# Half of the second layer's output projection moved into its attention, with the last two groups of heads taking turns

## The chip, the cores and the metric

The kernel runs on one core of a Trainium2 chip. The core has a matrix engine (TensorE, in the profile PE, with its weight loads as PEld), three engines for elementwise work (VectorE or DVE, ScalarE or ACT, GpSimd or POOL) and SyncE (SP), which here only issues DMAs. Every engine works through its own list of instructions in order; engines wait for each other by semaphores. The metric is the device time of one execution in microseconds (us).

## The reference

Four layers on an x of 2048 rows by 640 channels: attention, a state space convolution, attention, the convolution, each on a layer normalisation of x and each added to x. The attention has 32 heads of 20 channels.

```python
q, k, v = qkv[0], qkv[1], qkv[2]
scores = jnp.einsum("bhqd,bhkd->bhqk", q, k) * (Dh ** -0.5)
p = _softmax(scores, axis=-1)
o = jnp.einsum("bhqk,bhkd->bhqd", p, v)
return (lambda x, *d: x.transpose(*d))(o, 0, 2, 1, 3).reshape(B, S, D) @ wo
...
x = x + _A_ref(_layernorm(x, axis=-1), A_wqkv, A_wo)
x = x + _B_ref(_layernorm(x, axis=-1), B_log_A_real, B_A_imag, B_C_real, B_C_imag, B_log_dt, B_D_skip)
```

The product with wo is the output projection of the title: for each block of 128 rows, 640 channels of o (five channel tiles of 128) go into 640 columns, in two halves of 320.

## The kernel before, in words

**Attention** (`attention`, from L394) is made for two layers, one call each. The heads go in eight groups of four (L930), a group's queries in four blocks of 512 (L932), and for each block the keys in 16 tiles of 128 (L942). A key tile is two *scores* (L817: eight small matmuls on 64 x 32 pieces of PE's array, then one exponential of 128 x 1024 on ACT, L827, into `pt`) and one *values* (L833: the product of `pt` with V, summed in PSUM as `pa` over the 16 key tiles). A row of ones in V gives the softmax's denominator. There are 1024 exponentials in a layer.

At the end of a block of queries (L844 to L890) DVE adds the two halves of `pa` into `oc`; the denominators then go out and back: POOL stores them (`sums`, dn<-oc), loads them spread over the partitions (`load`, dr<-dn), DVE inverts them (`invert`), POOL stores and spreads them (`back`, dn<-dr; `spread`, db<-dn), DVE multiplies (`scale`) and POOL stores the result into `ot` in DRAM (`store`, ot<-oc). These steps are put off by planned times (L886: 0.2, 5, 10, 11 and 15.5 us after the block); `scale` comes when the next block of queries ends (L854).

Keys and queries are kept as operands in SBUF: `kop[j][half]` (two pairs of heads, two halves of the keys) and `qop[j][parity]`. `load_k` (L409) and `load_q` (L418) let SP load them from DRAM: the second half of the keys and the next queries at key tile 2 of a block (L949), the first half and the queries of the next group at key tile 10 of a group's last block (L955), after `need` has made sure that the group's projections are done.

**The order of the work** is set by a plan with a clock for PE, ACT and DVE (`Plan`, L50): scores cost PE 0.22 us and ACT 0.92 (L828), values cost PE 0.865 (L836). What is left of PE's time is filled from generators of small steps: `slot` (L672) takes the next step of `todo` when it fits before the planned end of the exponential under way less 0.5 us (L922). In the first layer a second source, the convolution's kernel (`pend`, from `kgen`), fills too; `AHEAD` (L33, L659) says how much of the first must be done at which exponential before the second is taken. The steps of `todo` are the projections of the other groups (`jobs`, L557: `qk` for queries and keys, `vq` for values, `both` to interleave them), and `fetch` (L605) loads the weights for them through one staging buffer `ws`: it turns what was staged into weights on DVE, and in the same call lets SP load the next. Within the attention each engine's order is fixed as written (`Ordered`, L62, and `chain`, L179, for PE). After it, instructions can be moved ahead of others on their engine.

When the projections are over, `end_jobs` (L892) frees their buffers, loads wo and lets POOL split it into two parts, `woh` and `wol` (`prefetch`, L972).

**The output projection** (`out_proj`, L1092) follows the attention: for each of 16 blocks of 128 rows, `out_split` (L994) loads the columns of `ot` (otl<-ot), rounds them (`oh`, on ACT) and takes the rest (`ol`, on DVE); 30 matmuls (two halves, five channel tiles, ol x woh, oh x woh, oh x wol) go to PSUM, and DVE adds the result to x. For two blocks at a time the layer normalisation follows (`ln_stats` L139, `ln_u` L1013): statistics and u on DVE, `uh` on ACT, `ul` on POOL. Then the convolution (`ssm`, L1128) begins with psx (L1163). Rows 12 to 15 belong to the last block of queries.

Of the kernel before, what the change touches and what calls it, by code (L numbers as in the profile page):

```python
# [32 lines left out]
AHEAD = ((0, 0.0), (110, 6.0), (236, 34.0), (364, 61.0), (600, 95.0), (740, 134.0))  # L33
# [51 lines left out]
def mha_s4d_kernel(ctx, tc, x_in, wqkv, wo, lar, aim, cr, ci, ldt, dsk,  # L85
# [48 lines left out]
    with tc.tile_pool(name="op", bufs=1) as op:  # L134
        oneh = op.tile([1, L], F16, name="oneh")
        ge.memset(oneh, 1.0)
        ge.dma_start(onesd, oneh)

# [255 lines left out]
    def attention(x, stats):  # L394
# [23 lines left out]
        def load_q(g, j, qb):  # L418

            qt = qop[j][qb % 2]  # L420
# [136 lines left out]
        def jobs():  # L557
# [59 lines left out]
            def vq(q):  # L617
                w = wv_.pop()
# [95 lines left out]
        with ExitStack() as c2:  # L714
# [82 lines left out]
            for j in range(2):  # L797
                load_k(0, j, 0)
                load_q(0, j, 0)
# [15 lines left out]
        ready, scaled = [], []  # L815
# [17 lines left out]
        def values(qb, g, kt, pts, pa):  # L833
# [10 lines left out]
            if kt == NI - 1:  # L844
# [9 lines left out]
                if scaled:  # L854
                    scaled.pop()()
# [26 lines left out]
                def store():  # L882
                    for j in range(4):
                        h = 4 * g + j
                        ge.dma_start(ot[h * DH:(h + 1) * DH, 512 * qb:512 * qb + 512], oc[32 * j:32 * j + DH, :])
                later.extend((plan.dve + n, f) for n, f in (  # L886
                    (0.2, sums), (5.0, load), (10.0, invert), (11.0, back), (15.5, spread)))
                later.extend((plan.dve + n, lambda: slow and slow.pop(0)[1]()) for n in (18.0, 21.0, 24.0))
                later.sort(key=lambda e: e[0])
                scaled.append(scale)  # L890
# [35 lines left out]

        last[0] = None
        tail = None
        every = {NBLK - 1, ("v", 3)}
        for g in range(H // 4):  # L930
            need(NEED[g], ("v", g // 2))
            for qb in range(4):  # L932
                if g == H // 4 - 1 and qb == 3:
                    if tail is None:
                        need(*every)
                        tail = end_jobs()
                    split, fetch = out_split(tail[-1], 1 if first_layer else 2)
                    first = []
                    later.extend(((plan.pe + 7.0, fetch), (plan.pe + 20.0, lambda: first.append(split(0)))))
                    later.sort(key=lambda e: e[0])  # L940
                pa = [pst("A", [P, 512], F32, tag=f"pa{r}", name=f"pa{r}") for r in range(2)]
                for kt in range(NI):  # L942
                    kc, pts = P * (kt % 8), []
                    for j in range(2):
                        pts.append(scores(kop[j][kt // 8], kc, qop[j][qb % 2]))
                        if j:
                            ready.append((plan.act, qb, g, kt, pts, pa))
                        fill(j)
                    if kt == 2:  # L949
                        for j in range(2):  # L950
                            if qb == 0:
                                load_k(g, j, 1)
                            if qb < 3:
                                load_q(g, j, qb + 1)
                    if qb == 3 and kt == 10 and g + 1 < H // 4:  # L955
                        need(NEED[g + 1])
                        for j in range(2):
                            load_k(g + 1, j, 0)
                            load_q(g + 1, j, 0)
                if tail is None and filler[0] is None and have.issuperset(every):  # L960
                    tail = end_jobs()
        for r_ in ready:
            values(*r_[1:])
        drain_later(True)
        scaled.pop()()
        drain_later(True)
        plan.keep = False
        first.append(split(1))
        c.close()
        return *tail[:-1], split, first  # L970
# [23 lines left out]
    def out_split(w2, n):  # L994

        def load(s):
            o = w2.tile([P, NCT, P], F32, name="otl")
            sy.dma_start(o, ot[:, s * P:s * P + P].rearrange("(t p) c -> p t c", p=P))
            return o
        o = []  # L1000

        def split(s):
            oh = w2.tile([P, NCT, P], F32R, name="oh")
            ol = w2.tile([P, NCT, P], F32R, bufs=n, name="ol")
            cur = o.pop(0)
            (ve.tensor_copy if s == 0 else se.copy)(oh, cur)
            ve.tensor_sub(ol, cur, oh)
            if s + 1 < NI:
                o.append(load(s + 1))
            return oh, ol  # L1010
        return split, lambda: o.append(load(0))

    def ln_u(x, i0, n, mvrs, uh, ul, pool):  # L1013
        mv, rs = mvrs
        for i in range(n):
# [76 lines left out]
    def out_proj(x, woh, wol, split, first, ln):  # L1092
        for s in range(NI):
            oh, ol = first.pop(0)
            pos = [pst("M", [P, 512], F32, tag="mm", name="po")[:, :320] for _ in range(2)]
            for hf in range(2):
                for ct in range(NCT):
                    te.matmul(pos[hf], ol[:, ct, :], woh[:, ct, 320 * hf:320 * hf + 320], start=(ct == 0), stop=False)  # L1098
            if s + 2 < NI:
                first.append(split(s + 2))  # L1100
            for hf in range(2):
                for ct in range(NCT):
                    for m in (woh, wol):
                        te.matmul(pos[hf], oh[:, ct, :], m[:, ct, 320 * hf:320 * hf + 320],  # L1104
                                  start=False, stop=(ct == NCT - 1 and m is wol))
                xs = x[:, s, 320 * hf:320 * hf + 320]
                ve.tensor_add(xs, xs, pos[hf])
                if s == 2:
                    weave(1000)
# [237 lines left out]
    def seq(x, general):  # L1347

        stats = None
        for n in range(0, len(parts), 2):  # L1350
            with ExitStack() as c:
# [4 lines left out]
                else:  # L1356
                    x, wc, *tail = attention(x, stats)
                psum(c, X=2)
# [9 lines left out]
                with ExitStack() as c2:  # L1368
                    up2 = c2.enter_context(tc.tile_pool(name="up2", bufs=2))

                    def ln(i0, m):
                        ln_u(x, i0, m, ln_stats(lambda i: x[:, i0 + i, :], m), uh, ul, up2)
# [97 lines left out]
```

## Time and profile before

| what | value |
|---|---|
| median of 3 runs | 2721.36 us (2717.77 to 2724.57) |
| the profiled execution | 2718.84 us |
| its span, first to last instruction | 2717.1 us |
| PE busy | 2534.4 us (93% of the span) |
| ACT busy | 2337.4 us (86%) |
| DVE busy | 1477.0 us (54%) |
| POOL busy | 852.6 us (31%) |
| exponentials of the first layer | 115.5 to 1099.8 us |
| exponentials of the second layer | 1503.5 to 2485.5 us |
| second layer's output projection on PE | 2488.3 to 2558.8 us |

Rows of the profile name a line, an engine, an operation and its operands as out<-in; a number in brackets is the time that the engine stood idle before, with the engine that ended it. L77 is the line of the helper `Ordered`, which issues most instructions of ACT, DVE, POOL and SP, so these are told apart by their operands. SPq and POOLq rows are DMA issues.

### The profile page before, as it was taken

The numbers are of one execution on the slowest core, as the hardware profiler recorded it, in microseconds if no ns is written. First come the engines' busy times: TensorE is split into PE (matmuls) and PEld (weight loads), VectorE is DVE, ScalarE is ACT, GpSimd is POOL, SyncE is SP. The second block draws the span as 40 slices with busy tenths as digits, with TensorE's granted clock in tenths as the row PEclk, the third lists the DMA queues.
The fourth block names the chain that finished last, engine by engine and source line by source line (L and its number), as shares of the span: only waits on it lengthen the run. The fifth ranks groups of instructions, "written<-read, shape, count | busy, mean of one in ns | idle before, by whom it ended". The sixth has DMA issues, their size and how long they took to land.

```text
span 2717.1 us, 115609 instructions
## 1 busy us (share of the span) xinstructions
PE 2534.4 (93%) x50944; PEld 1445.2 (53%) x50944; DVE 1477.0 (54%) x3292; ACT 2337.4 (86%) x2762; POOL 852.6 (31%) x1282
## 2 busy tenths in 40 slices
PE   7899999999999988999999999899999998888998
PEld 3445444444444433777886445444445443335988
DVE  7777877778856970577776332232232220003865
ACT  7899999999999999455655899899999999997464
POOL 1132333333333343301670122222223223222376
PEclk9999999999999999999999999999999999999999
DMA  6522222232222232455542111111121112112365
GB/s 214 174 62 75 63 77 64 73 75 61 65 51 59 51 112 87 145 210 194 178 142 67 45 52 52 50 53 46 46 66 35 50 36 61 41 38 80 110 191 161
DMA packets 183153, 238.55 MB, mean 88 GB/s; under 512 B 42737, under 2 KB 128241, under 8 KB 180849
## 3 DMA queue, kind: packets, MB, share of 16 engines
q1 hardware_dynamic: 146304, 184.48, 21.0%
q0 software_dynamic: 36336, 46.59, 7.2%
q8 instruction: 402, 6.59, 1.0%
q14 instruction: 111, 0.90, 0.1%
HBM read 154.90 MB, written 76.03 MB: 85 GB/s over the span
## 4 chain that ended last, share of the span: by engine, by line
ACT 49%; PE 30%; issue 9%; DVE 7%; DMA 4%; POOL 1%; SPq 0%; ACTq 0%; DVEq 0%; POOLq 0%
ACT pt L77 47%; PE pa L841 5%; PE S L824 3%; PE psv L1198 3%; PE po L1104 3%; PE psy L1208 2%; PE m L578 2%; PE psx L1186 2%; PE psx L1163 2%; PE po L1098 1%; PE pst L1173 1%; PE pkf L1078 1%; DMA kop<-ks 1%; PE pv L544 1%; PE pq L730 1%
## 5 line engine op out<-in xcount | busy, mean ns | idle before, releaser
L77 ACT ACTIVATE pt<-S 128x1024 f32<-128x1024 f32 x2048 | 1922.9, 1037 | 46.7 <-PE S L824 37.1
L841 PE MATMUL pa<-pt,V 64*32 64x512 f32 x16384 | 1101.0, 590 | 0.9 <-DVE oc L77 0.8
L824 PE MATMUL S<-qop,kop 61*32 61x512 f16 x16384 | 880.4, 381 | 125.4 <-ACT pt L77 105.1
L824 PEld LDWEIGHTS <-kop 61*32 61x32 f16 x16384 | 375.1, 89 | 784.1 <-issue 660.0
L841 PEld LDWEIGHTS pa<-pt,V 64*32 64x32 f32 x16384 | 315.0, 106 | 69.9 <-DVE oc L77 6.6
L77 POOL DMA_DIRECT2D dn<-oc x256 | 126.7, 501 | 700.9 <-DVE oc L77 644.7
L77 DVE COPY oc<-pa 128x512 f32<-128x512 f32 x64 | 44.2, 690 | 312.1 <-PE pa L841 307.2
L77 DVE TENSOR_SCALAR qc<-m 128x512 f32<-128x512 f32 (+1 forms) x68 | 46.9, 689 | 296.4 <-PE m L578 296.4
L77 POOL DMA_DIRECT2D db<-dn x256 | 130.0, 513 | 111.6 <-DMA dn<-dr 107.7
L578 PE MATMUL m<-xh,wh 64*32 64x512 f16 x2560 | 146.7, 379 | 1.4 <-DVE qc L77 1.4
L578 PE MATMUL m<-xh,wl 64*32 64x512 f16 x2560 | 147.3, 378 | 0.0
L578 PE MATMUL m<-xl,wh 64*32 64x512 f16 x2560 | 145.5, 377 | 0.0
L77 POOL DMA_DIRECT2D ot<-oc x256 | 130.2, 516 | 12.7 <-issue 8.3
L578 PEld LDWEIGHTS <-wh 64*32 64x32 f16 x5120 | 92.5, 94 | 74.1 <-issue 32.6
L1191 POOL TENSOR_TENSOR t<-t,kb 128x512 f32<-128x512 f32 x80 | 102.0, 1276 | 72.3 <-DVE t L77 58.2
L77 ACT COPY xt<-pst 128x1024 f16<-128x1024 f16 x80 | 81.5, 1022 | 47.6 <-PE pst L1173 47.5
L77 POOL DMA_DIRECT2D dn<-dr x64 | 35.8, 559 | 257.5 <-DVE dr L77 237.1
L544 PEld LDWEIGHTS <-xh 128*128 128x128 f16 x960 | 79.6, 98 | 50.9 <-issue 35.6
L77 DVE TENSOR_TENSOR kb<-ktab 128x512 f32<-128x512 f32 x160 | 106.3, 682 | 0.0
L77 DVE TENSOR_SCALAR V<-m 128x160 f32<-128x160 f32 x64 | 20.7, 324 | 156.3 <-PE m L544 156.3
L77 DVE TENSOR_SCALAR dr<-dr 128x16 f32<-128x16 f32 x64 | 11.0, 171 | 171.8 <-DMA dr<-dn 171.6
L1020 POOL TENSOR_TENSOR ul<-u,uh 128x640 f16<-128x640 f32 x30 | 46.1, 1555 | 177.7 <-ACT uh L77 177.7
(269 smaller groups left out, 4045.7 us busy)
## 6 DMA issues: line engine op xcount, KB each, us to landing
ka<-kha SPq DMA_DIRECT2D x80, 256.0 KB
kb<-khb SPq DMA_DIRECT2D x80, 256.0 KB
db<-dn POOLq DMA_DIRECT2D x256, 64.0 KB, 2.7
kpw<-wd POOLq DMA_DIRECT2D x60, 192.0 KB, 4.8
qop<-qs SPq DMA_DIRECT2D x256, 40.0 KB
kop<-ks SPq DMA_DIRECT2D x128, 80.0 KB
ot<-oc POOLq DMA_DIRECT2D x256, 40.0 KB, 2.3
otl<-ot SPq DMA_DIRECT2D x32, 320.0 KB
```

The source lines that it names most:

```text
L77: made = f(out, *a, **k)
L544: chain(te.matmul(ps[:, :n], a_[:, ct, sl], m[:, ct, :], start=(k == 0), stop=(k == 14)))
L578: chain(te.matmul(ps[r][32 * t:32 * t + 32, :], a_[rows, ct, 32 * u:32 * u + 32], m[rows, ct, 512 * v:512 * v + 512], start=(k == 0), stop ...
L824: chain(te.matmul(S[32 * t:32 * t + 32, 512 * r:512 * r + 512], kt_[rows, kc + 32 * t:kc + 32 * t + 32], qt[rows, :], start=True, stop=Tru ...
L841: chain(te.matmul(pa[r][32 * j:32 * j + 32, :], V[rows, kt, VP * h:VP * h + 32], pts[j // 2][rows, 512 * (j % 2):512 * (j % 2) + 512], sta ...
L1020: (ve if s == NI - 1 else ge).tensor_sub(ul[:, s, :], u, uh[:, s, :])
L1104: te.matmul(pos[hf], oh[:, ct, :], m[:, ct, 320 * hf:320 * hf + 320], start=False, stop=(ct == NCT - 1 and m is wol))
L1163: te.matmul(ps[:, r, i, :], e1[:, e, s, r, :], m[:, s, bs], start=(n == 0), stop=(n == 2))
L1186: te.matmul(px, f2[:, f, :], xt[:, k, :], start=(n == 0), stop=(n == 2))
L1191: ge.tensor_mul(t2, t2, kb)
L1198: te.matmul(pv[:, g].rearrange("p r i c -> p (r i c)"), t1[:, g * P:g * P + P], fa, start=True, stop=True)
L1208: te.matmul(py[:, i, :], eb[:, 4 * i4 + i, r, :], v[:, r, 4 * i4 + i].rearrange("p g c -> p (g c)"), start=(r == 0), stop=(r == 1))
```

## The change

1. *Turns.* In the second layer the last eight blocks of queries go (group 6, block 0), (group 7, block 0), (group 6, block 1) and so on. Keys are reloaded at each change of group; the next group is asked for at key tile 8, not 10, in both layers, and `AHEAD` is moved to fit.
2. *Storing.* In these eight, `scale` comes 22 us after the block and not at the end of the next.
3. *Rows.* A class `Rows` takes the place of `out_split`. In the second layer a block of rows can be done in two items, channel tiles 0 to 2 and 3 to 4. Once the projections are over, the generator `rows_out` fills PE's gaps with these items, four matmuls a step: an item is loaded by SP, split by DVE, multiplied in the PSUM banks that the projections used, and added to x by DVE. An item of tiles 3 and 4 may go when both last groups have stored the block of queries. When both items of a row block are done, its statistics are taken at once (`stats_of`).
4. *After the attention* `out_proj` does what is left. For row blocks that are whole, the normalisation uses the statistics that are there and makes u on ACT.
5. *Staging.* `fetch` no longer loads the next weights in the call that turns the staged ones into weights, and `vq` has an empty first step.

```diff
-AHEAD = ((0, 0.0), (110, 6.0), (236, 34.0), (364, 61.0), (600, 95.0), (740, 134.0))
+AHEAD = ((0, 0.0), (110, 6.0), (236, 32.0), (364, 59.0), (600, 95.0), (724, 134.0))
...
-                if order and (order[0][0] == "v" or not ws_):
+                elif order and (order[0][0] == "v" or not ws_):
...
             def vq(q):
+                yield 0.0, 0.0, False, ()
...
-                if scaled:
-                    scaled.pop()()
+                while scaled:
+                    scaled.pop(0)()
...
+                if first_layer or g < H // 4 - 2:
+                    scaled.append(scale)
+                else:
+                    later.append((plan.dve + 22.0, scale))
...
+        class Rows:
...
+            def load(self, item):
+                s, c0, c1 = item
+                o = self.w2.tile([P, NCT, P], F32, name="otl")
+                sy.dma_start(o[:, c0:c1], ot[c0 * P:c1 * P, s * P:s * P + P].rearrange("(t p) c -> p t c", p=P))
+                self.loaded.append((item, o))
...
+            def pick(self):
+                for c in (3, 0):
+                    for item in self.left:
+                        s, c0, c1 = item
+                        if c0 == c and (c == 0 or all(4 * g + s // 4 in stored for g in (H // 4 - 2, H // 4 - 1))):
+                            self.left.remove(item)
+                            return item
+
+        def rows_out(rows, x, woh, wol):
...
+                (s, c0, c1), oh, ol = rows.split(ve.tensor_copy)
+                t0, t = plan.dve + 0.2, ask()
+                mm = [(hf, a, m, ct) for hf in range(2) for ct in range(c0, c1) for a, m in ((ol, woh), (oh, woh), (oh, wol))]
...
+                    part_ = mm[k:k + 4]
+                    cost = 0.25 + 0.147 * len(part_)
+                    yield t0, cost, k > 0, tuple(hf for hf in range(2) if k <= half * hf < k + 4)
...
+                        evac = lambda: ve.tensor_add(xs, xs, pos[hf])
+                        emptied(*((None, evac) if hf else (evac,)))
+                if s in parts_done:
+                    stats_of(x, s, rows.mv[:, s, :])
+                    rows.whole.add(s)
+                parts_done.add(s)
...
+        turns = [(g, qb) for g in range(NG) for qb in range(4)]
+        if not first_layer:
+            turns[-8:] = [(g, qb) for qb in range(4) for g in (NG - 2, NG - 1)]
...
+            if tail is not None and rows is None and (n == len(turns) - 1 or not first_layer):
+                rows = Rows(tail[-1], 1 if first_layer else 2)
...
+                    todo[0], head[0] = rows_out(rows, tail[0], tail[2], tail[3]), None
...
+                        if n == 0 or turns[n - 1][0] != g:
+                            load_k(g, j, 1)
+                        if g2 == g and qb2:
+                            load_q(g, j, qb2, n + 1)
+                if kt == 8 and g2 != g:
+                    need(NEED[g2])
+                    for j in range(2):
+                        load_k(g2, j, 0)
+                        load_q(g2, j, qb2, n + 1)
...
-            ve.tensor_scalar(u, x[:, s, :], mv[:, i, 0:1], rs[:, i:i + 1], ALU.subtract, ALU.mult)
+            if on_act:
+                se.activation(u, x[:, s, :], AF.Identity, scale=rs[:, i:i + 1], bias=nb[:, i:i + 1])
+            else:
+                ve.tensor_scalar(u, x[:, s, :], mv[:, i, 0:1], rs[:, i:i + 1], ALU.subtract, ALU.mult)
...
+                        if not general and rows.whole >= set(range(i0, i0 + m)):
+                            mv = rows.mv[:, i0:i0 + m, :]
+                            ln_u(x, i0, m, (mv, rstd(mv, m)), uh, ul, up2, True)
+                            return
```

More of the change, by code (lines that the diff above doesn't have):

```diff
@@ L798, in attention @@
                 load_k(0, j, 0)
[L799 removed]
+                load_q(0, j, 0, 0)
             values4(3)
@@ L927, in attention @@
         last[0] = None
-        tail = None
+        tail, rows, stop = None, None, []
         every = {NBLK - 1, ("v", 3)}
-        for g in range(H // 4):
-            need(NEED[g], ("v", g // 2))
[L932 to L937, printed above, removed]
-                    first = []
[L939 to L943, printed above, removed]
-                    for j in range(2):
[L945 to L961, printed above, removed]
@@ L962, in attention @@
         for r_ in ready:
             values(*r_[1:])
+        if not first_layer:
+            stop.append(True)
+            first = []
+            while head[0] is not None and head[0][1]:
+                slot()
+            for s in range(NI):
+                two = [(s, 0, 3), (s, 3, NCT)]
+                if set(two) <= set(rows.left):
+                    rows.left = [e for e in rows.left if e not in two] + [(s, 0, NCT)]
         drain_later(True)
-        scaled.pop()()
-        drain_later(True)
+        while scaled:
+            scaled.pop(0)()
+            drain_later(True)
@@ L967, in attention @@
         plan.keep = False
-        first.append(split(1))
         c.close()
-        return *tail[:-1], split, first
+        return *tail[:-1], rows, first
     def prefetch(x, rest):
@@ L992, in prefetch, with ln_u @@
         return x, c, woh, wol, c.enter_context(tc.tile_pool(name="wo2", bufs=2, side="right"))
[L994 to L1013, printed above, removed]
+    def ln_u(x, i0, n, mvrs, uh, ul, pool, on_act=False):
         mv, rs = mvrs
+        if on_act:
+            nb = sm.tile([P, n], F32, name="nb")
+            ve.scalar_tensor_tensor(nb, mv[:, :, 0], -1.0, rs, ALU.mult, ALU.mult)
         for i in range(n):
```

120 lines of the change are left out of this document (99 added, 21 removed).

## The prediction

> **What bounds the kernel now.** I read the busy times by stage first, then the chain of waits, then the timeline at each place that the diff touches. Three rows of stages for the second attention (quarters of 256 exponentials; PE and ACT alone, scores and exponentials), then two rows with all engines: stage, length, busy us and count of PE, weight loads, DVE, ACT, POOL, then clock, DMA share, GB/s.
>
> ```profile
> 1751.80:2003.00 251.20, 109.55 (x2048) 241.53 (x256) 0.98 0.18 53
> 2003.00:2248.50 245.50, 113.00 (x2048) 240.53 (x257) 1.00 0.17 48
> 2248.50:2485.50 237.00, 107.20 (x2040) 236.43 (x257) 1.00 0.15 41
> ...
> 2220.00:2460.00 240.00, 194.72 (x4173) 80.69 (x4161) 22.89 (x53) 239.94 (x262) 71.78 (x130) 1.00 0.16 44
> 2490.00:2570.00 80.00, 77.61 (x609) 76.64 (x609) 67.97 (x178) 29.06 (x50) 31.88 (x30) 1.00 0.33 102
> ```
>
> The last quarter is the last two groups of heads. It takes 237.0/256 = 0.926 us per exponential and ACT is never idle: ACT is the bound, PE has only scores and values left, DVE works 23 of 240 us. In the output projection after it PE works 77.6 of 80 us and DVE 68.0: PE bounds it, with DVE close behind.
>
> PE's room shows in one key tile of the last groups, which is two exponentials long:
>
> ```profile
> 2300.52 0.41 PE L824 MATMUL S<-qop,kop 61*32 61x512 f16 x8 [0.35 <-ACT pt L77]
> 2300.74 1.05 PE L841 MATMUL pa<-pt,V 64*32 64x512 f32 x16
> 2301.59 0.41 PE L824 MATMUL S<-qop,kop 61*32 61x512 f16 x8
> 2302.35 0.41 PE L824 MATMUL S<-qop,kop 61*32 61x512 f16 x8 [0.34 <-ACT pt L77]
> ```
>
> Start to start, scores take 0.22 and values 0.85. From 2301.59 to 2302.35 PE has 0.76 - 0.22 = 0.54 us free of 1.83. Over the 128 key tiles of the two groups that is 69 us.
>
> The projection itself, on the chain of waits:
>
> ```profile
> 2489.97 2.93 PE po L1104 x20
> ...
> 2494.37 2.93 PE po L1104 x20
> ...
> 2558.75 0.23 PE L1163 MATMUL psx<-uh,e1s 128*128 128x128 f16 x1
> ```
>
> A block of rows takes 4.40 us, its 30 matmuls 0.147 each, and nothing else is between the blocks. Sixteen are 70.4 us and end at 2558.75.
>
> **The change part by part.** *Rows within the attention.* A block of rows is cut into 18 matmuls (channel tiles 0 to 2) and 12 (tiles 3 and 4). They are issued four at a time, with a planned 0.838 us, when that ends 0.5 us before the planned end of the exponential under way. Worked through with the plan's constants (scores 0.22, values 0.865, exponential 0.92), this gives one step in two key tiles: 64 steps or 256 of the 480 matmuls, if it begins with group 6. First halves go first; the second halves of a block of queries may go once both last groups have stored it, some 24 us (13 key tiles) after its end. At 9 key tiles for a first half and 6 for a second, the eight turns hold seven first halves and ten second ones: rows 0 to 6 whole, 228 matmuls (33.5 us) left for later. What PE needs is 256 x 0.147 = 38 us and the switching, out of 69 free.
>
> The switching is seen where the value projection, also over 128 rows of the array, is woven in:
>
> ```profile
> 1906.14 0.41 PE L824 MATMUL S<-qop,kop 61*32 61x512 f16 x8
> 1906.48 0.24 PE L544 MATMUL m<-vh,xl 128*128 128x160 f16 x1
> ...
> 1906.91 0.23 PE L544 MATMUL m<-vh,xl 128*128 128x160 f16 x1
> 1907.07 0.41 PE L824 MATMUL S<-qop,kop 61*32 61x512 f16 x8
> ```
>
> Scores to these is 0.34, where scores to values was 0.22; they follow each other by 0.07, and the next scores come 0.16 after the last. An excursion costs 0.12 + 0.09 = 0.2 us, 64 of them 13: 38 + 13 = 51 of 69, hidden. [...]
>
> The splits, additions and statistics of seven rows fall to a DVE that works 23 of 240 us, so they cost nothing while it isn't held up (next but one). Yet a filled quarter is slower than an empty one: 245.5 against 237.0, of which 2.6 is one wait shown below; 5.9 in seven filled blocks is 0.85 each. Eight would be 6.8; these steps leave PE more air, so I take **+5** (0 to +14, the other filled quarter).
>
> *The projection after the attention.* PE's 70.4 us shrink to 33.5, but now the division of the last block of queries ends last. POOL's issues for it, and the time to landing:
>
> ```profile
> 2488.41 1.94 POOL L77 DMA_DIRECT2D dn<-oc  x4 [18.83 <-DVE oc L77]
> ...
> 2501.03 2.02 POOL L77 DMA_DIRECT2D db<-dn  x4 [1.40 <-DMA dn<-dr]
> 2504.92 3.23 POOL L1020 TENSOR_TENSOR ul<-u,uh 128x640 f16<-128x640 f32 x2 [1.87 <-ACT uh L77]
> 2508.11 2.03 POOL L77 DMA_DIRECT2D ot<-oc  x4
> ...
> ot<-oc POOLq DMA_DIRECT2D x256, 40.0 KB, 2.3
> ```
>
> The store lands at 2508.1 + 2.0 + 2.3 = 2512.4. Row 12 is then loaded (taken as 2.3 too), cast and subtracted (0.73 + 0.85, below) and begins near 2516.5, where it was 2541. Rows 7 to 11, some 17 us of PE, are done before. Rows 12 to 15 keep 4 x 4.40 = 17.6, so PE ends at 2534.5 in place of 2558.75: **-24**. The normalisation of the last rows and the next layer follow as before.
>
> ```profile
> L77 DVE TENSOR_TENSOR x<-x,po 128x320 f32<-128x320 f32 x31 | 15.0, 483 | 7.0 <-PE po L1104 6.8
> L77 DVE TENSOR_TENSOR ol<-otl,oh 128x640 fp32r<-128x640 f32 x14 | 11.9, 853 | 0.4
> L77 ACT CAST oh<-otl 128x640 fp32r<-128x640 f32 x14 | 10.2, 726 | 26.8 <-PE po L1104 13.7 <-issue 12.4 <-ACT uh L77 0.7
> L77 ACT ACT_TABLE_LOAD x1 | 1.3, 1283 | 0.0
> ```
>
> DVE does not take PE's place: a whole row needs neither of its two rows here nor its statistics, and u goes to ACT (two passes of about 0.73 for seven rows, 10 us, beside PE). POOL's subtractions, 1.6 each, stand between the issues of the division: up to 4 us later, or 3 earlier if none is ahead of the store. A square root drawn between exponentials would cost two table loads, 2.6. So -28 to -17.
>
> *Where the rows begin.* The output weights are made on POOL at the same moment, and the sums of the block before queue behind them:
>
> ```profile
> 2258.94 1.55 POOL L989 TENSOR_TENSOR wol<-wot,woh 128x640 fp32r<-128x640 f32 x1 [9.61 <-issue]
> ...
> 2269.14 2.16 POOL L77 DMA_DIRECT2D dn<-oc  x4
> ...
> 2276.81 0.17 DVE L77 TENSOR_SCALAR dr<-dr 128x16 f32<-128x16 f32 x1 [24.46 <-DMA dr<-dn]
> ```
>
> Group 6 begins at 2248.5; six us for the load and about two for the split bring PE to the first weights near 2256.5, and they are ready at 2260.5. DVE stands at dr until 2276.8, which so far delayed nothing; now the emptying of PSUM and the next split are queued behind it, and PE, whose order is fixed, behind these. Two waits of 3 to 5 us, less some 1.5 each that the two score buffers cover: **+5** (0 to +15).
>
> *Taking turns.* Keys and queries change at seven turns, where the last two groups had one change. SP's issues at that one:
>
> ```profile
> 2350.04 2.28 SPq L77 DMA_DIRECT2D kop<-ks  x4
> ...
> 2361.98 0.25 SPq L77 DMA_DIRECT2D qop<-qm  x1
> 2364.70 2.29 SPq L77 DMA_DIRECT2D kop<-ks  x4
> ```
>
> SP starts when key tile 7 frees the first halves of the keys and needs 12.2 us for twenty issues. With some 2.3 to landing they are there at 2364.5, just as the last scores of the block before free the second halves (2364.70): no spare. The second halves have until key tile 8. The rows' own loads (0.36 us of issue each) share this queue, but those that wait for a store come after key tile 12 by the plan, behind these twenty. 0.4 a turn: **+3** (0 to +35, a rival below).
>
> *SP's queue elsewhere.* Asking for the next group at key tile 8, not 10, and staging weights one unit later take a hold away:
>
> ```profile
> 1739.13 0.83 DVE L77 SCALAR_TENSOR_TENSOR wl<-ws,wh 128x640 f16<-128x640 f32 x1
> 1739.99 0.40 SPq L77 DMA_DIRECT2D ws<-in_wqkv  x1
> 1742.33 2.31 SPq L77 DMA_DIRECT2D kop<-ks  x4
> 1751.78 1.02 ACT L77 ACTIVATE pt<-S 128x1024 f32<-128x1024 f32 x1 [2.83 <-PE S L824]
> 1758.22 1.02 ACT L77 ACTIVATE pt<-S 128x1024 f32<-128x1024 f32 x1 [5.42 <-PE S L824]
> 2127.92 4.04 ACT L77 ACTIVATE pt<-S 128x1024 f32<-128x1024 f32 x4 [2.57 <-PE S L824]
> L77 ACT ACTIVATE pt<-S 128x1024 f32<-128x1024 f32 x2048 | 1922.9, 1037 | 46.7 <-PE S L824 37.1
> ```
>
> SP waited for DVE to leave the staging buffer (wl) while the keys of the next group stood behind; ACT then idled 2.83 + 5.42, and 2.57 at another change. I take 8 of these 10.8 as gone, and 2 of the smaller waits in the first layer (46.7 in both layers together): **-10** (-16 to +6, since a block of projections that is forced two key tiles sooner can also stall ACT). The first layer's output rows are loaded and split as before.
>
> Sum: -24 + 5 + 5 + 3 - 10 = **-21**. The profiled execution took 2718.84 (the span of 2717.1 and 1.7 around it), 2.5 under the median of 2721.36. That gives 2697.8 by its own time and **2700** against the median.
>
> **The rivals.** *Given back at the start and the turns.* The waits behind the weights at their upper end (+15) and 1 us a turn (+7), in place of +5 and +3: -7, 2714. For it: DVE's idle 24 us are real, and a fixed order now hangs on them. Against: the rows have two PSUM banks, so one wait of DVE isn't at once one of PE.
>
> *Keys late at every turn (the slower side).* The place is SP's queue between key tile 7 and the next block. A row load that stands there waiting for its store (2.0 of issue and 2.3 of landing), or slower landings, shift all twenty. There is no spare, so each us costs seven: at 5 us a turn, 35 in place of 3, it is +11, 2732. It decides from 21/7 + 0.4 = 3.4 us a turn. For it: 8.3 us were lost at 1751 because one queue was held. Against: the plan's order, and a DMA share of 0.15.
>
> [...]
>
> [...]
>
> [...]
>
> *Nothing given back.* Filling, start and turns cost 1 together: -24 + 1 - 10 = -33, 2688.
>
> **How the numbers follow.** Forecast 0.55 (2690 to 2711), given back 0.15, keys late 0.13, drain 0.05, nothing given back 0.12. A measurement of this kernel tells about 0.3%, 8.2 us, from no change, so faster is under 2713.2. Faster: 0.55 + 0.12 + 0.05, a third of given back = 0.72. Same: 0.10 + 0.05 + 0.02 = 0.17. Slower: 0.11. The range of 2684 to 2721 holds the forecast, given back, the drain and over half of the best case: 0.82.
>
> **What would show it.** Right: about 256 output matmuls between scores from 2250 on; the last two groups in 245 to 255 us where they took 237; ACT idle at most 1 us at a turn; row 12's first matmul some 31 us after the last exponential; no wait of several us as group 2 of the second layer begins. Wrong: under 40% or over 60% of the projection woven in; ACT idle by several us at each turn; row 12 held past 36 us, by POOL or otherwise; or new waits in the first layer, where I count on almost nothing.

## The result, and the profile after

The changed kernel takes 2735.32 us (median of 6 runs, 2732.62 to 2738.44), the kernel before 2721.2 in the same measurements. The ratio is 1.0049, with a 95% interval of 1.0036 to 1.0062: **slower by 0.5%**, where 2700 had been forecast, and outside the range of 2684 to 2721. Among the experiments below, one of the four runs of the kernel without turns took 3627.12 us, at a granted clock of 0.654, and is left out of its median.

The profiled execution spans 2734.0 us (before: 2717.1). Cut at the first and the last exponential of each layer, and at the first exponential of the last two groups of heads, the two executions stand like this (us):

| stretch | before | after | difference |
|---|---|---|---|
| up to the first exponential | 115.5 | 114.9 | -0.6 |
| first attention | 984.3 | 987.2 | +2.9 |
| projection, convolution and what leads to the second attention | 403.7 | 403.9 | +0.2 |
| second attention up to group 6 | 745.1 | 733.1 | -12.0 |
| last two groups, eight blocks of queries | 236.9 | 279.2 | **+42.3** |
| from the last exponential to the end | 231.6 | 215.6 | -16.0 |
| sum | 2717.1 | 2734.0 | +16.9 |

The gains that were looked for came, though the last is short of its 24; the last two groups took all of them back and more. Here are the three last quarters of the second attention in the changed kernel, as shown of before (stage, length, PE and ACT in scores and exponentials, clock, DMA share, GB/s):

```profile
1750.60:1996.50 245.90, 112.08 (x2048) 241.58 (x257) 1.00 0.20 54
1996.50:2239.20 242.70, 112.64 (x2048) 240.96 (x257) 1.00 0.17 48
2239.20:2518.40 279.20, 108.41 (x2040) 244.17 (x257) 0.95 0.23 64
```

The quarter that had been the quickest is the slowest now, and it is the only one where the granted clock is under 1.00. The next rows are three of its eight turns with all engines: the first, the third and the fifth.

```profile
2239.25:2284.42 45.17, 30.41 (x535) 13.04 (x535) 5.14 (x11) 30.46 (x34) 17.91 (x24) 0.85 0.25 73
2315.39:2346.53 31.14, 30.02 (x547) 13.75 (x547) 4.70 (x10) 30.46 (x34) 7.08 (x14) 1.00 0.24 62
2377.37:2412.49 35.12, 31.02 (x541) 13.57 (x541) 9.07 (x29) 33.25 (x36) 7.09 (x14) 0.95 0.21 58
```

A block of queries took 29.5 us before. The first turn takes 45.2, turns two to four about 31.0 each, turns five to eight 35.1 to 35.5 each. So there are three sizes of loss. In the first turn ACT works 30.5 of 45.2 us: it waits. In the third it works nearly all the time. In the fifth it works 33.25 us for the same number of exponentials: something else ran on it.

*The first turn.* The chain of waits of the changed kernel, where the rows begin:

```profile
2255.62 1.53 POOL wol L1090
...
2257.17 0.39 SPq L77
...
2258.86 1.05 DMA kop<-ks
...
2260.30 0.57 DVE ol L77
...
2260.96 1.41 PE m L995 x4
```

SP's DMA at 2257.17 is the first load of a row block (otl). It was issued 0.02 us after POOL had finished the last part of the output weights. SP's own waits between 2236 and 2262 (us in total, times, longest) say for what it stood, and its timeline which load it was:

```profile
SPq L77 <- POOL wol L1090: 13.2, 1, 13.2
...
2257.17 0.39 SPq L77 DMA_DIRECT2D otl<-ot  x1
```

In `prefetch` the pool of the row tiles (`wo2`) is opened just after that of the weights' staging tiles (`wos`) is closed, and POOL reads the staging tiles until 2257.15. So the loaded tile lies, by this order, in memory that the staging tiles had before; the addresses themselves are in no view. DVE's split waits for the load, PE for the split. (The chain puts DVE's wait down to a load of keys that landed at the same time; the split reads the row tile alone.) I had looked at the weights and at DVE's inversion as what PE would wait for, and took the load itself as done in six us.

PE stood still for 12.4 us meanwhile, and this is how it starts again (timeline of PE, start and length in us, idle time before in brackets):

```profile
2260.96 0.61 PE L995 MATMUL m<-woh,ol 128*128 128x320 f32 x1 [12.44 <-DVE ol L77]
2261.37 0.47 PE L995 MATMUL m<-woh,oh 128*128 128x320 f32 x1
2261.64 0.47 PE L995 MATMUL m<-wol,oh 128*128 128x320 f32 x1
```

The same matmuls follow each other by 0.27 us instead of 0.147. The granted clock of this turn is 0.85 on average: 0.50 from 2260.96 to 2265.0, with 0.27 us between these matmuls, and 1.00 from 2265.0 to 2268.0, where those of the next step are 0.15 apart.

*Turns five to eight.* The timeline of ACT in the fifth turn:

```profile
2391.11 1.28 ACT L77 ACT_TABLE_LOAD   x1
2392.41 0.20 ACT L77 ACTIVATE lt<-va 128x2 f32<-128x2 f32 x1
2392.63 1.28 ACT L77 ACT_TABLE_LOAD   x1
2393.93 2.95 ACT L77 ACTIVATE pt<-S 128x1024 f32<-128x1024 f32 x3
2397.78 1.02 ACT L77 ACTIVATE pt<-S 128x1024 f32<-128x1024 f32 x1 [0.91 <-PE S L831]
```

This is the square root of a pair of row blocks that are whole. It belongs to the normalisation after the attention, but its inputs are ready and nothing ties it there, so it was placed between two exponentials: a table load for the root, the root, a table load back, 2.8 us from exponential to exponential. PE stands idle for 2.6 of them and then has the slower clock again (0.50 from 2395.0 to 2397.0, 1.00 from 2398.6 to 2402.0), with 0.27 us between matmuls:

```profile
2395.00 0.73 PE L831 MATMUL S<-qop,kop 61*32 61x512 f16 x8 [2.58 <-ACT pt L77]
...
2396.09 0.47 PE L995 MATMUL m<-woh,oh 128*128 128x320 f32 x1
2396.36 0.47 PE L995 MATMUL m<-wol,oh 128*128 128x320 f32 x1
```

ACT waits for scores another 0.91 and 0.37. The other three turns have one root each, also between two table loads of 1.28 us.

*After the last exponential* (2518.4) the last block's division is what ends last, as forecast, but later. POOL in the changed kernel:

```profile
2522.51 1.96 POOL L77 DMA_DIRECT2D dn<-oc  x4 [8.50 <-DVE oc L77]
...
2530.87 2.75 POOL L1108 TENSOR_TENSOR ul<-u,uh 128x640 f16<-128x640 f32 x2
2535.19 0.56 POOL L77 DMA_DIRECT2D dn<-dr  x1 [1.57 <-DVE dr L77]
2535.78 2.77 POOL L1108 TENSOR_TENSOR ul<-u,uh 128x640 f16<-128x640 f32 x2
2538.50 2.00 POOL L77 DMA_DIRECT2D db<-dn  x4
...
2545.89 2.03 POOL L77 DMA_DIRECT2D ot<-oc  x4 [2.57 <-DVE rs L77]
```

The low parts of the eight whole rows (ul) stand between the steps of the division. The store (ot) goes out 27.5 us after the last exponential, where it was 22.6 before; row 12's first matmul comes at 37.9 and not at 31. The first of the last four row blocks also takes 7.0 us in place of 4.4: PE had waited 6.96 us before it, and up to 2561.86 its matmuls follow each other by 0.27 us, at a granted clock of 0.50.

### The profile page after: what moved, and what is told of

It is laid out like the page before. It is cut to its first block, busy times and chain, and to the rows that moved or that the text cites. A ratio compares the mean times of both kernels' runs of the same rounds, so it can differ in the third digit from the quotient of the medians.

```text
span 2734.0 us, 115884 instructions
## 1 busy us (share of the span) xinstructions
PE 2555.3 (93%) x50944; PEld 1442.4 (53%) x50944; DVE 1498.9 (55%) x3334; ACT 2357.2 (86%) x2772; POOL 849.1 (31%) x1282
## 4 chain that ended last, share of the span: by engine, by line
ACT 48%; PE 26%; issue 12%; DVE 8%; DMA 4%; POOL 1%; SPq 0%; ACTq 0%; DVEq 0%; POOLq 0%
ACT pt L77 48%; PE pa L848 4%; PE S L831 3%; PE psv L1296 3%; PE psy L1306 2%; PE po L1202 2%; PE psx L1284 2%; PE psx L1261 2%; PE m L584 1%; PE pst L1271 1%; DMA kop<-ks 1%; PE pkf L1166 1%; PE po L1197 1%; PE pkx L1149 1%; DVE ktab L77 1%
## 5 line engine op out<-in xcount | busy, mean ns | idle before, releaser
L831 PEld LDWEIGHTS <-kop 61*32 61x32 f16 x16384 | 366.1, 89 | 755.1 <-issue 630.0
L77 DVE TENSOR_SCALAR V<-m 128x160 f32<-128x160 f32 x64 | 20.7, 323 | 161.7 <-PE m L550 161.7
L77 DVE TENSOR_TENSOR x<-x,m 128x320 f32<-128x320 f32 x34 | 16.5, 487 | 157.1 <-PE m L995 157.0
L1290 POOL TENSOR_TENSOR t<-t,t 128x512 f32<-128x512 f32 x78 | 99.2, 1271 | 7.3 <-DVE t L77 1.3
```

The lines of the kernel that those rows point to most:

```text
L77: made = f(out, *a, **k)
L831: chain(te.matmul(S[32 * t:32 * t + 32, 512 * r:512 * r + 512], kt_[rows, kc + 32 * t:kc + 32 * t + 32], qt[rows, :], start=True, stop=Tru ...
L1290: (ge if g0 else ve).tensor_add(t1, t1, t2)
```

## The experiments

Times are medians; each kernel was timed against the kernel before on the same chip, and ratios are to that. Stage times are from each kernel's profiled execution.

**No square root before the last exponential.** In the function `rstd`, and its call for whole rows:

```diff
-        se.activation(t, va, AF.Sqrt)
+        made = se.activation(t, va, AF.Sqrt)
+        if after is not None:
+            tie(made, after)
...
-ln_u(x, i0, m, (mv, rstd(mv, m)), uh, ul, up2, True)
+ln_u(x, i0, m, (mv, rstd(mv, m, after=se.last)), uh, ul, up2, True)
```

> The changed kernel with one tie more: the square root of the row blocks that are whole may not come before the attention's last exponential. Theory (table loads): the four square roots that stand between exponentials cost 2.9 us each and about 1 us more because PE, idle meanwhile, then runs slowly; all four go, -12 to -16 us, some 2720, and turns 5 to 8 cost 1.5 us each over an empty block as turns 2 to 4 do. Rival (weaving): the last four turns are 5.5 us dearer because of their second halves and their waits for stores; -4 us or less, over 2731.

Measured: 2713.93 us, ratio 0.9971 (0.9959 to 0.9984), 21 under the changed kernel. The last two groups, in one row:

```profile
2236.20:2500.90 264.70, 107.15 (x2040) 243.83 (x257) 0.97 0.24 67
```

264.7 in place of 279.2; turns five to eight now take 30.9 to 31.3 each, as turns two to four do. So the 4 us that set them apart were the square roots, and the second halves and their stores cost nothing of their own. The two profiled executions differ by 21.4 us: 14.5 in this stage (16.7 less in turns five to eight, 2.1 more in the first turn, whose wait is still there), 3.8 after the last exponential (211.8 in place of 215.6), and 3 in stages that the edit doesn't touch.

The remaining 1.5 us a turn are seen in the same run. PE's timeline around one step of four matmuls:

```profile
2331.40 0.51 PE L833 MATMUL S<-qop,kop 61*32 61x512 f16 x8
2331.84 0.41 PE L997 MATMUL m<-woh,ol 128*128 128x320 f32 x1
2332.09 0.31 PE L997 MATMUL m<-woh,oh 128*128 128x320 f32 x1
...
2332.63 0.41 PE L833 MATMUL S<-qop,kop 61*32 61x512 f16 x8
```

From scores to scores 1.23 us. Scores alone are 0.22 and four matmuls 4 x 0.147 = 0.59, so going over to them and back costs 0.42, twice what I had read from the value projection (0.2). The plan allows 0.838 for a step that takes 1.01. Most of the exponentials that follow a step start some 0.16 us late, against the usual 0.92 from start to start; in each of turns two to eight nine to twelve exponentials are late, by 1.5 to 2.0 us together (two to four before, by 0.2 to 0.4, but for the last turn). In sum PE still has room (64 x 0.42 + 38 = 65 of 69 us), but not at each place.

**The first load 22 us later**, after the weights are made:

```diff
+            yield plan.pe + 22.0, 0.0, False, ()
             t, done, parts_done = ask(), [], set()
```

> The changed kernel with the first load of a row block 22 us later in the plan, after the output weights have been split. Theory (shared buffer): the first load waits for POOL to finish the weights since it gets the memory of their staging, and PE stands 12.4 us for it; the wait of 13.5 us in the first turn goes, -13 us, some 2722, with some 24 matmuls fewer within the attention. Rival (DVE held): the wait moves to DVE's inversion of the denominators, which comes late because POOL was busy; -3 us at most, over 2731.

Measured: 2710.24 us, ratio 0.9955 (0.9941 to 0.9969), 25 under the changed kernel. The last two groups:

```profile
2236.20:2497.90 261.70, 109.07 (x2040) 243.50 (x257) 0.97 0.24 67
```

The first turn falls from 45.2 to 29.7 us. In this run DVE's wait for the late denominators, 25.8 us, stands in front of the first split, and no exponential of the first turn waits. The edit puts off the matmuls together with the load, so it shows that the loss hangs on where the rows begin; which wait it was is read from SP's wait above. Three square roots still stand between exponentials in this run, and its end takes 211.5 us, 4 less than in the changed kernel.

**The queue's edits alone**: the kernel before with `need` and the loads at key tile 8, the moved `AHEAD`, and the staging one unit later.

```diff
-        if not first_layer:
+        if False:
             turns[-8:] = [(g, qb) for qb in range(4) for g in (NG - 2, NG - 1)]
...
-            if tail is not None and rows is None and (n == len(turns) - 1 or not first_layer):
+            if tail is not None and rows is None and n == len(turns) - 1:
...
-                if first_layer:
+                if True:
                     later.extend(((plan.pe + 7.0, lambda: rows.load(rows.left.pop(0))),
...
-        if not first_layer:
+        if False:
             stop.append(True)
```

Rows are then left whole, as in the first layer, and begin with the last block of queries; the division stores as before.

> The kernel before with only the earlier request of the next group (key tile 8), the moved plan line and the later staging of weights: no rows within the attention, no turns, storing as before. Theory: the second attention up to group 6 gains the 12 us that the changed kernel gains there, the first attention loses 2; some 2711. Rival: the gain there belongs to what comes after, or is paid back in the first layer; 2718 or more.

Measured: 2707.23 us, ratio 0.9942 (0.9926 to 0.9959), and 2706.92 with 0.9951 (0.9937 to 0.9965) when it was run again (below). Two quarters of its second attention:

```profile
1751.67:1997.91 246.24, 112.48 (x2048) 241.74 (x258) 1.00 0.20 54
1997.91:2240.60 242.69, 112.75 (x2048) 240.94 (x258) 1.00 0.18 48
```

246 and 243 where the kernel before had 251 and 245.5, and the quarter ahead of them takes 244.3 in place of 248.3: the 12 us of the changed kernel come from these edits alone, and what follows is as before (236.9 and 230.4). The three waits at the changes to groups 2 and 5 are gone. So this small part of the diff is faster than the whole by 28 us. Which of its three edits removed the waits was not separated.

**Turns and early storing, no rows within the attention:**

```diff
-            if tail is not None and rows is None and (n == len(turns) - 1 or not first_layer):
+            if tail is not None and rows is None and n == len(turns) - 1:
...
-                if first_layer:
+                if True:
                     later.extend(((plan.pe + 7.0, lambda: rows.load(rows.left.pop(0))),
...
-        if not first_layer:
+        if False:
             stop.append(True)
```

Rows are left whole here too.

> The changed kernel with no rows within the attention: turns and early storing stay, the whole projection is done after the attention. Theory: with the keys just in time a turn costs under 0.5 us, the last two groups take 237 to 241 us; some 2714. Rival (keys late at each turn): 3 us or more a turn, 258 us or more, 2732 or more.

Measured: 2713.33 us, ratio 0.9976 (0.9966 to 0.9985). The last two groups:

```profile
2237.30:2479.30 242.00, 110.41 (x2040) 237.16 (x257) 0.99 0.24 66
```

Seven turns take 29.5 to 29.8 us, 0.1 over a block without them. The last one takes 34.5: a cast of the first row block stands between its exponentials and holds them for 3.6 us. Keys and queries come in time at each turn, so the rival of late keys, whose 2732 lies close to the measured time, is refuted: its place costs nothing.

**Both repairs together**, in the changed kernel:

```diff
+            yield plan.pe + 22.0, 0.0, False, ()
...
-ln_u(x, i0, m, (mv, rstd(mv, m)), uh, ul, up2, True)
+ln_u(x, i0, m, (mv, rstd(mv, m, after=se.last)), uh, ul, up2, True)
```

> The changed kernel with both repairs: no square root before the last exponential, and the first load 22 us later. Theory: the two add up; the last two groups take 30 us in the first turn and 31.0 in each of seven others, 247 (279 in the changed kernel), and what follows the last exponential some 210; 2735 - 21 - 22 = 2692, to 2696. Rival (one wait hides the other): no better than the better of the two alone, 2710.

Measured: 2704.07 us, ratio 0.9943 (0.9926 to 0.9959), 31 under the changed kernel and short of the 39 to 43 hoped for. The last two groups do what was expected:

```profile
2236.70:2484.80 248.10, 107.60 (x2040) 243.02 (x257) 1.00 0.25 70
```

The end does not: 216.4 us in place of 210. The last exponential ends at 2484.8. DVE in this run, with POOL's rows beneath:

```profile
2501.71 2.98 DVE L77 TENSOR_TENSOR lt<-lt,va 128x2 f32<-128x2 f32 x1
...
2505.99 4.87 DVE L77 TENSOR_TENSOR ol<-otl,oh 128x640 fp32r<-128x640 f32 x2
...
2515.44 0.49 DVE L77 TENSOR_TENSOR x<-x,po 128x320 f32<-128x320 f32 x1 [4.05 <-PE po L1205]
2515.84 0.68 DVE L77 TENSOR_TENSOR oc<-oc,db 128x512 f32<-128x512 f32 x1
```

```profile
2501.90 2.76 POOL L1111 TENSOR_TENSOR ul<-u,uh 128x640 f16<-128x640 f32 x2
...
2506.68 2.76 POOL L1111 TENSOR_TENSOR ul<-u,uh 128x640 f16<-128x640 f32 x2
```

An operation on 128 x 2 elements, 0.16 us elsewhere, takes 2.98, and ends with POOL's pair of subtractions; two splits take 4.87 in place of 1.6, across the next pair. The multiplication of the division (oc<-oc,db) comes 31 us after the last exponential, where the kernel before has it at 20. In DVE's order it stands behind an addition to x, and that one waited 4.05 us for PE, whose products need the late splits. That DVE's long operations come from POOL's subtractions is read from the times alone; in the changed kernel the same operation takes 2.93 us, from 2530.72, beside the pair on POOL that is shown at 2530.87 above.

**The low parts of whole rows on DVE:**

```diff
-            (ve if s == NI - 1 else ge).tensor_sub(ul[:, s, :], u, uh[:, s, :])
+            (ve if on_act or s == NI - 1 else ge).tensor_sub(ul[:, s, :], u, uh[:, s, :])
```

> As with both repairs, and the low parts of the whole rows (ul) are made on DVE, so that they no longer stand on POOL between the steps of the last block's division. Theory (POOL holds the division): the store of the last block comes 23 us after the last exponential and not 27.5, row 12 at 33 and not 36.5; -3 to -4 us against both repairs, 2688 to 2690. Rival (DVE then holds it, or the DMAs' landing does): within 1 us of both repairs.

Measured: 2695.3 us, ratio 0.9908 (0.9891 to 0.9924), 9 under both repairs alone, which is over twice the expected gain. Run again (below) the ratio is 0.9920, 6 us under both repairs. Of the 8.2 us between the two profiled executions 6.1 lie after the last exponential, which is what the edit touches. POOL after the last exponential, which ends at 2482.7 here:

```profile
2497.02 0.56 POOL L77 DMA_DIRECT2D dn<-dr  x1 [2.19 <-DVE va L77]
2499.51 2.00 POOL L77 DMA_DIRECT2D db<-dn  x4 [1.94 <-DMA dn<-dr]
...
2507.78 2.02 POOL L77 DMA_DIRECT2D ot<-oc  x4
```

The store goes out at 25.1 us after it (32.0 with both repairs alone), row 12 begins at 35.0 (41.2), and the end takes 210.3.

**No turns, with both repairs** (the last two groups one after the other):

```diff
-        if not first_layer:
+        if False:
             turns[-8:] = [(g, qb) for qb in range(4) for g in (NG - 2, NG - 1)]
```

> As with both repairs, but the last two groups of heads are done one after the other as before the change. Theory: a turn costs 0.1 us, and the second halves of the first rows still find room as group 7 goes on, so nothing changes: 2692 to 2697. Rival A (turns are needed): fewer rows are whole, more work is left after the last exponential; 2700 or more. Rival B (turns are what costs 1.4 us each): 2684.

Measured: 2701.63 us, ratio 0.9934 (0.9914 to 0.9954). The last two groups:

```profile
2236.50:2482.30 245.80, 105.96 (x2040) 242.58 (x257) 1.00 0.17 46
```

2.3 us less than with turns, and 30.6 to 31.1 a block from the second on. Fewer row blocks become whole (four, against seven with turns), as the first rival said, but the time is no longer for it. So the turns cost next to nothing and give nothing; 1.4 us a block belongs to the weaving.

**Three matmuls in a step:**

```diff
-                    part_ = mm[k:k + 4]
-                    cost = 0.25 + 0.147 * len(part_)
+                    part_ = mm[k:k + 3]
+                    cost = 0.40 + 0.147 * len(part_)
...
-                    yield t0, cost, k > 0, tuple(hf for hf in range(2) if k <= half * hf < k + 4)
+                    yield t0, cost, k > 0, tuple(hf for hf in range(2) if k <= half * hf < k + 3)
```

> As with both repairs, but three matmuls in a step with a planned fixed cost of 0.40 in place of four with 0.25 (0.84 us planned for either). Theory (a switch costs 0.42 us): a step of four takes 1.0 us and puts off one exponential by 0.16, 1.4 us a turn; with three it takes 0.86, and a turn costs 0.3 us or less over an empty one. The last two groups take 239 us, a quarter fewer matmuls are woven in, and the division still ends after the rest: -7 us, 2685. Rival (the waiting in a turn comes from DVE or from the keys): the turns stay at 31.0, 2692 or more.

Measured: 2703.62 us, ratio 0.9936 (0.9920 to 0.9953), no different from four a step. The last two groups:

```profile
2240.40:2483.60 243.20, 107.54 (x2040) 240.38 (x257) 1.00 0.26 69
```

The stage gains 4.9 us, and turns two to five take 30.1 to 30.3. That is as the dearer switch would have it, though 0.6 and not 0.3 over an empty block, and turns six and seven stay at 31. There the trace has one wait of ACT for scores, of 0.60 us in each, and without it they would be near the others; PE had waited 0.28 us just before for a split that DVE made ahead of emptying `pa`, but that this is the cause is not shown. But 312 matmuls were left for the end (258), where row 12 began at 45.9 us: here the rows, not the division, came last. It is half a proof: the steps' length matters, and the end took the gain.

**No turns, and the low parts of whole rows on DVE**, with both repairs:

```diff
-        if not first_layer:
+        if False:
...
-            (ve if s == NI - 1 else ge).tensor_sub(ul[:, s, :], u, uh[:, s, :])
+            (ve if on_act or s == NI - 1 else ge).tensor_sub(ul[:, s, :], u, uh[:, s, :])
```

> Both repairs, the low parts of whole rows on DVE, and no turns: the last two groups one after the other. Theory (turns give nothing): with both repairs alone the run without turns was 2 us faster; here again within 3 us of the 2695 with turns, likely 2692. Rival (turns let more rows be whole, which counts once the division is no longer held): 2699 or more.

Measured: 2701.05 us, ratio 0.9919 (0.9905 to 0.9932). It can't be told from the version with turns (0.9908, and 0.9920 when run again).

**All low parts before row 12 on DVE**, in the kernel of the run above, without turns:

```diff
-            (ve if on_act or s == NI - 1 else ge).tensor_sub(ul[:, s, :], u, uh[:, s, :])
+            (ve if on_act or low or s == NI - 1 else ge).tensor_sub(ul[:, s, :], u, uh[:, s, :])
...
-ln_u(x, i0, m, ln_stats(lambda i: x[:, i0 + i, :], m), uh, ul, up2)
+ln_u(x, i0, m, ln_stats(lambda i: x[:, i0 + i, :], m), uh, ul, up2, low=n > 0 and i0 < 12)
```

> As the run without turns, with the low parts of all rows before 12 on DVE, so that POOL does nothing but the division's DMAs until its store. Theory (POOL): the store comes another 1 to 2 us sooner, near 23 us after the last exponential, row 12 near 33; 1 to 2 us faster than with the whole rows' alone. Rival (DVE): 0.8 us more on DVE for each of some five rows puts off its multiplication by the spread denominators; no gain or some us slower.

Measured: 2700.28 us, ratio 0.9925 (0.9911 to 0.9938). The store comes at 23.3 us (24.6 in the run above) and row 12 at 34.7 (35.0): what was left on POOL no longer matters.

**The best version beside the queue's edits alone**, on one chip; both are kernels shown above (turns, both repairs and the low parts on DVE; and the queue's edits), with no further edit.

> The kernel with both repairs, turns, and the low parts of whole rows on DVE, once more, beside the kernel with the queue's edits alone. Theory (weaving pays once its two waits are gone): stages say 248 + 210 against 237 + 230.5 for the last two groups and what follows, so it is 9 us faster than the queue's edits alone, 12 at most: 2695 to 2699. Rival (the queue's edits are all of the gain, and weaving only shifts work): within 3 us of the other, 2704 or more.

> The queue's edits alone, beside the kernel with both repairs and the low parts on DVE. Theory: 2706 to 2708, 9 to 12 us slower than that one. Rival: the same time as that one within 3 us.

Measured: 2698.06 us, ratio 0.9920 (0.9906 to 0.9933), against 2706.92. What the whole diff has beyond the queue's edits, the weaving above all, is worth 9 us, once its two waits and POOL's subtractions between the steps of the division are gone. This version beats both kernels: 0.8% under the kernel before, and some 1.3% under the changed one.

## Why the prediction was wrong

Point by point, with the working's own terms, forecast against measured (us):

| step | forecast | measured |
|---|---|---|
| the queue elsewhere | -10 | -12.0 in the second layer; the first attention 2.9 longer |
| turns | +3 | under +1 (seven of 0.1) |
| weaving | +5 | about +12 (1.5 a turn) |
| where the rows begin | +5, to +15 | about +14 |
| square roots between exponentials | 2.6, once, only in the range | about +16 (four of 4) |
| after the last exponential | -24 | -16 |

**What held.** ACT bounds the last two groups, and PE has the room for half of the projection: 252 of 480 matmuls were woven in, where 256 had been counted. The 228 that were left are the number of the prediction, but by luck: its seven first halves and ten second ones are 246 and leave 234; the kernel did eight and nine. The queue's hold was real and the edits took it away in the second layer, by 12 us where 8 was taken. The other 2, taken as gained in the first layer, were not: with these edits the first attention takes 984.1 to 988.3 us, 986.6 on average over thirteen profiles, against 984.3 in the one profile of before. The division of the last block does end last after the change. Turns bring their keys in time.

**What failed, by size of the error.** First, the square roots. The prediction names one, "drawn between exponentials", prices it at 2.6 us and puts it into an end of a range. It should have been a term of the sum. The row blocks become whole two by two within the attention, so four pairs had a root ready while exponentials still ran, and the order on ACT was free for what belongs to the time after. The root with its pair of loads is 2.8 us from exponential to exponential, and what follows, with PE at a granted clock of 0.50, is more than another 1 (ACT's waits of 0.91 and 0.37 in the fifth turn). Taking them away gave 21 us in all, of which 16.7 lie in the four turns.

Second, where the rows begin. The mechanism that I named, DVE standing at the late denominators, cost nothing visible; the loss came with a load that waited 13.2 us for POOL. The weights were read too early as well: the row shown with "ready at 2260.5" is the first of five such parts, and the last two in the kernel before are

```profile
2266.15 3.04 POOL L989 TENSOR_TENSOR wol<-wot,woh 128x640 fp32r<-128x640 f32 x2
```

so POOL was done at 2269.2, 20.7 us after group 6 began (17.9 in the changed kernel). The upper end of 15 happened to hold the size, but not its reason, and the sum took a third of it.

Third, the division. I saw the subtraction that stood before the store and allowed 4 us of delay; the term taken was that of the kernel before, where few rows reach POOL so early. With eight rows whole, POOL's subtractions stood between the steps, and a DVE operation of 0.16 us took 2.93 beside them; in the run with both repairs, with fewer whole rows, it took 2.98, and the multiplication came 11 us later than before. That the store had room to come at 25 us is shown by moving the low parts.

Fourth, weaving. A switch took 0.42 us where 0.2 had been forecast, a value at which PE just does not bound (64 switches into the 31 us that its 38 leave of 69 are 0.48 each). The drain to which the chances give 0.05 is shown by no run; what the runs show is the 0.42 us. By the sum the dearer switch stayed hidden; by the place of each step it did not, which the sum over a stage can't see.

The rival of the slower side gave 2732, close to the measured 2735, but by late keys, which the run with turns alone refutes. It was right by its number only. Of the signs set out beforehand, the last two groups (279.2 us where 245 to 255 was said) and row 12 (37.9 us, past 36) spoke against the forecast.

What stays open: the waits of 0.60 us in turns six and seven with three matmuls a step, and why a switch costs 0.42 us here and 0.2 at the value projection, whose matmuls differ in type, in width and in the time to load their weights (98 ns there, 188 here). Not separated either is how much of the start's 14 us is the wait and how much the slow clock after it.

## What to carry to other kernels

When work is moved ahead, look at what comes after it and becomes ready with it: an instruction that is free to move can go to where its inputs are ready, and here, where it needed another table on ACT, each cost two loads of 1.28 us and a while of PE's slower clock (0.50 for 2 us in the fifth turn), 4 us in all. A load has to be followed back to the memory that it is put into: here it waited 13.2 us for POOL, which, by the order of the pools, read the buffer's former content. And a stage that is filled to its room should be planned with the measured length of a step, not with the sum over the stage.

## What the hardware showed that was not expected

PE ran at about half speed after waits of 12.4, of 7.0 and of 2.6 us (0.27 us between matmuls in place of 0.147, at a granted clock of 0.50), and in the turns with such waits the granted clock was 0.85 and 0.94 to 0.95; so these stalls of PE cost more than their length. Going from small pieces of the array to the whole and back cost 0.42 us with the 32-bit weights of the output projection, against 0.2 with the 16-bit ones of the value projection. A DVE operation of 0.16 us took 2.93 and 2.98 us in two runs beside POOL's subtractions.
